# Windowed attention feeding a highway layer on one core: early v-buffer init, early sink rows, weights behind blocks 4 and 5, x of 15 blocks transposed by TensorE

## The chip, the core and the metric

The kernel runs on one core of a Trainium2 chip. Its time is the device time of one execution, in microseconds (us); a kernel's figure is the median of its runs. A run counts as slow when it is more than 1.5% above the fastest run of the same kernel. The profile is one execution. Its span, from the first to the last instruction, was about 1.7 us shorter than the time of the same execution.

## The reference

```python
# q, k, v: [4 batches, 8 heads, 768 positions, 64], float32; n_sink = 4, window = 128
scores = (q @ k.T) / 8
keep   = (key position < 4) | (0 <= query position - key position < 128)
a      = softmax(where(keep, scores, -1e9))
x      = (a @ v), heads side by side          # [3072 tokens, 512]
H, T   = relu(x @ w_h), sigmoid(x @ w_t + b_t)
out    = T * H + (1 - T) * x                  # [3072, 512], float32
```

The kernel cuts the tokens into 24 blocks of 128, six to a batch. A block needs its own keys and values, those of the block before, and the four "sink" keys and values at the start of the batch. Blocks 0 and 1 of a batch have the sinks inside their window, so the separate sink product starts at the third block of each batch (blocks 2, 8, 14, 20).

## The kernel before

TensorE (PE), VectorE (DVE), ScalarE (ACT), GpSimd (POOL) and SyncE (SP) each run their own list of instructions in order. An instruction that must wait holds back everything behind it in its list; the timeline of the kernel before, below, shows a memset that waits 9.3 us and the work held behind it. PSUM is the memory into which TensorE's products go in this kernel; "the crossbar" stands for a transpose made by a DMA transfer (`dma_start_transpose`), which SyncE issues.

GpSimd issues the loads of q, k and v, which convert to 16 bits on the way, and it also does small pieces of work on the sinks:

```python
NV = AHEAD + 4                                   # AHEAD = 8
v_ring = [const.tile([P, VW], FP16, ...) for i in range(NV)]      # 12 v buffers

# VectorE, at the very start
for vt in v_ring[0:3]:
    init_v(vt)                                   # the column of twos and the padding

# GpSimd, at the start:  loads 0, 1, 2 among the masks, then
load_v(2)
load_sink_v(0)
load_qk(3); load_v(3)
nc.gpsimd.dma_start(out=wt_sb, ...)              # the two weights
nc.gpsimd.dma_start(out=wh_sb, ...)
load_qk(4); load_v(4)
```

The main loop is a software pipeline. In iteration i it works on several blocks:

```python
for i in range(-2, NB + LAG + 1):                # LAG = 4, NB = 24
    m, o = i - LAG, i - LAG - 1
    if i == -2:
        warm_up(8); more_constants(); late_constants()
        for vt in v_ring[3:NV]:
            init_v(vt)                           # VectorE
        sink_ones(); sink_v(0)                   # sink_v: GpSimd makes the sink values
    act_sink(i)                                  # ACT, third block of a batch on, every second i
    pe_S(i + 1, 0); act_S(i + 1, 0); pe_S(i + 1, 1)     # scores, exp
    dve_d(o); dve_mask(i, 1)
    pe_T(i + 2)                                  # PE transposes q and k
    dve_e(o)
    pe_A(i)                                      # attention product, sinks included
    act_T(i + 2)                                 # ACT copies the transposes out of PSUM
    act_S(i + 1, 1); dve_mask(i + 1, 0)
    dve_rec(i); dve_o(o)                         # one reciprocal a block
    dve_x(i); sp_X(i)                            # x, and its transpose by DMA (crossbar)
    pe_Mt(m); act_u(m); pe_Mh(m)                 # the two highway products
    pe_sink(i + 1)                               # sink scores, every second i
    for n in ...: load_qk(n); load_v(n)          # 5 to 8 at i = -2, then n = i + 10
    if on(i + 2) and (i + 2) % NSC == 0:
        pool_sink((i + 2) // NSC)                # GpSimd: sink keys
    if i % NSC == 3: load_sink_v(i // NSC + 1)
    if i > 0 and i % NSC == 0: sink_v(i // NSC)  # GpSimd: sink values
# (conditions shortened)
```

The transposes of q and k, the highway products and the sink scores share two PSUM buffers, in rotation (`m_ps`, two buffers).

The softmax here doesn't subtract the row's maximum and nothing guards it: scores larger than these inputs give would overflow.

## Time and profile before

| | before |
|---|---|
| median of runs | 148.12 us (147.62 to 149.33, four runs) |
| span of the profile | 144.5 us |
| PE / DVE / ACT / POOL busy | 76 / 67 / 60 / 52% |
| reciprocal of block 0, block 4, block 23 | 29.2, 47.1, 128.5 us |

The reciprocals are good milestones: there is one a block, right after the block's attention product. The profiled run was a quick one (146.2 us of device time); over all calls the kernel before ranged from 145.8 to 152.3 us.

The page of the kernel before gives, under "busy tenths in 40 slices", how busy each engine was in each fortieth of the span (3.6 us), and further down the chain of work that ended last, as shares of the span:

```profile
PE   6645000190799999989999994899999999979930
DVE  6220000464066789988888995499889989988990
POOL 6989980399999959876746479641030000000000
DMA v<-in_v_dram 21%; POOL qsd L83 8%; POOL ksd L84 7%; PE tps L313 7%; PE hps L326 6%; POOL v L91 6%; PE av L279 6%; PE sps L245 3%; DVE dd L332 3%; DVE ee L338 2%; DVE otok L344 2%; ACT e L253 2%; PE av L285 2%; POOL vs L129 2%; PE tps L311 2%
```

PE is idle for long stretches up to slice 10 (36 us) and almost full from slice 12 on (slice 25 holds the longer of two waits for sink values). The list of waits (engine and line, what ended the wait, us in total, number of waits, longest) names the holes:

```profile
DVE v L94 <- DMA v<-in_v_dram: 18.4, 2, 9.3
PE av L279 <- DVE e L264: 15.5, 2, 14.7
PE sk L223 <- POOL ks L214: 4.4, 1, 4.4
PE av L285 <- POOL vs L129: 3.3, 2, 2.6
```

The timeline of the same kernel (start, duration, engine, line, operation, and in brackets the idle time before it with what ended it) shows the order:

```profile
17.56 0.95 POOL L91 DMA_DIRECT2D v<-in_v_dram  x1
18.17 0.07 DVE L94 MEMSET v<- 128x8 f16 x1 [9.34 <-DMA v<-in_v_dram]
27.27 0.07 DVE L94 MEMSET v<- 128x8 f16 x1 [9.01 <-DMA v<-in_v_dram]
28.24 0.93 PE L279 MATMUL av<-v,e 128*128 128x112 f16 x8 [14.72 <-DVE e L264]
36.96 1.03 PE L223 MATMUL sk<-qk,ks 128*128 128x128 f16 x8 [4.36 <-POOL ks L214]
47.13 0.21 DVE L293 RECIPROCAL rec<-av 128x8 f32<-128x8 f32 x1
```

Loads 3 and 4 were written in the program before the init of the buffers they fill, so the memsets had to wait until the loads landed: twice 9 us. The masks stand behind the memsets in VectorE's list, and the attention product behind the masks.

### The profile page before, as it was taken

The numbers are of one execution on the slowest core, as the hardware profiler recorded it, in microseconds if no ns is written. First come the engines' busy times: TensorE is split into PE (matmuls) and PEld (weight loads), VectorE is DVE, ScalarE is ACT, GpSimd is POOL, SyncE is SP. The second block draws the span as 40 slices with busy tenths as digits, with TensorE's granted clock in tenths as the row PEclk, the third lists the DMA queues.
The fourth block names the chain that finished last, engine by engine and source line by source line (L and its number), as shares of the span: only waits on it lengthen the run. The fifth ranks groups of instructions, "written<-read, shape, count | busy, mean of one in ns | idle before, by whom it ended". The sixth has DMA issues, their size and how long they took to land.

```text
span 144.5 us, 3130 instructions
## 1 busy us (share of the span) xinstructions
PE 109.9 (76%) x1216; PEld 70.4 (49%) x1216; DVE 97.0 (67%) x213; ACT 86.9 (60%) x105; POOL 75.8 (52%) x99
## 2 busy tenths in 40 slices
PE   6645000190799999989999994899999999979930
PEld 2234000180688566656765663567666666644400
DVE  6220000464066789988888995499889989988990
ACT  3058300061499869887886989198869888812210
POOL 6989980399999959876746479641030000000000
PEclk9999999999999999999999999999999999999998
DMA  1999999999999999999999999999943422634331
GB/s 11 111 134 105 119 173 169 86 96 147 160 156 155 153 134 194 196 186 163 179 187 187 182 185 161 140 178 195 185 119 109 113 90 79 54 111 128 126 145 73
DMA packets 92784, 20.14 MB, mean 139 GB/s; under 512 B 88673, under 2 KB 89697, under 8 KB 92770
## 3 DMA queue, kind: packets, MB, share of 16 engines
q0 software_dynamic: 76256, 10.51, 116.2%
q1 hardware_dynamic: 16514, 9.44, 31.3%
q8 instruction: 9, 0.15, 0.5%
q14 instruction: 5, 0.04, 0.1%
HBM read 21.01 MB, written 6.29 MB: 189 GB/s over the span
## 4 chain that ended last, share of the span: by engine, by line
PE 29%; POOL 25%; DMA 21%; issue 9%; DVE 8%; ACT 4%; POOLq 0%; DVEq 0%
DMA v<-in_v_dram 21%; POOL qsd L83 8%; POOL ksd L84 7%; PE tps L313 7%; PE hps L326 6%; POOL v L91 6%; PE av L279 6%; PE sps L245 3%; DVE dd L332 3%; DVE ee L338 2%; DVE otok L344 2%; ACT e L253 2%; PE av L285 2%; POOL vs L129 2%; PE tps L311 2%
## 5 line engine op out<-in xcount | busy, mean ns | idle before, releaser
L253 ACT ACTIVATE e<-sps,ebias 128x1024 f16<-128x1024 f32 (+1 forms) x48 | 49.8, 1042 | 19.8 <-PE sps L245 19.6
L279 PE MATMUL av<-v,e 128*128 128x112 f16 x352 | 25.4, 221 | 15.5 <-DVE e L264 15.5
L264 DVE TENSOR_TENSOR e<-e,mask 128x1024 f16<-128x1024 f16 (+1 forms) x48 | 31.1, 650 | 7.5 <-ACT e L253 7.1
L279 PEld LDWEIGHTS <-e 128*128 128x128 f16 x352 | 21.3, 102 | 21.0 <-DVE e L264 16.6
L205 ACT COPY qk<-tp 128x1024 f16<-128x1024 f16 x24 | 24.1, 1003 | 7.0 <-PE tp L200 7.0
L91 POOL DMA_DIRECT2D v<-in_v_dram x24 | 21.8, 910 | 10.2 <-DVE v L94 6.4
L84 POOL DMA_DIRECT2D ksd<-in_k_dram x24 | 21.7, 902 | 6.8 <-PE tps L313 3.4
L83 POOL DMA_DIRECT2D qsd<-in_q_dram x24 | 22.2, 925 | 4.9 <-DMA ksd<-in_k_dram 1.4
L326 PE MATMUL hps<-wh_sb,xT 128*128 128x512 f16 x96 | 24.6, 379 | 0.0
L313 PE MATMUL tps<-wt_sb,xT 128*128 128x512 f16 x96 | 24.6, 379 | 0.0
L319 ACT ACTIVATE u<-tps 128x512 f16<-128x512 f32 x24 | 14.4, 599 | 14.6 <-PE tps L313 14.6
L332 DVE SCALAR_TENSOR_TENSOR dd<-hps,xh 128x512 f16<-128x512 f32 x24 | 16.6, 690 | 7.4 <-PE hps L326 7.0
L245 PE MATMUL sps<-qk 64*128 64x128 f16 x352 | 16.0, 231 | 2.7 <-ACT qk L205 2.2
L338 DVE SCALAR_TENSOR_TENSOR ee<-u,dd 128x512 f16<-128x512 f16 x24 | 16.5, 686 | 0.5
L298 DVE TENSOR_TENSOR xh<-av,rec 128x512 f16<-128x512 f32 x24 | 16.4, 685 | 0.2
L245 PEld LDWEIGHTS <-qk 64*128 64x128 f16 x352 | 11.2, 100 | 9.9 <-issue 7.8
L344 DVE SCALAR_TENSOR_TENSOR otok<-xh,ee 128x512 f32<-128x512 f16 x24 | 15.6, 652 | 0.2
L326 PEld LDWEIGHTS <-xT 128*128 128x128 f16 x96 | 9.4, 98 | 11.8 <-issue 0.8
L313 PEld LDWEIGHTS <-xT 128*128 128x128 f16 x96 | 9.4, 98 | 9.2
L94 DVE MEMSET v<- 128x8 f16 x12 | 0.7, 65 | 18.4 <-DMA v<-in_v_dram 18.4
L285 PE MATMUL av<-vs,es 128*128 128x260 f16 x32 | 9.0, 281 | 3.3 <-POOL vs L129 3.3
L200 PE MATMUL tp<-ident,ksd 128*128 128x128 f16 x96 | 10.5, 238 | 1.1 <-DMA ksd<-in_k_dram 1.1
(45 smaller groups left out, 81.4 us busy)
## 6 DMA issues: line engine op xcount, KB each, us to landing
out_dram<-otok SPq DMA_DIRECT2D x24, 256.0 KB, 3.8
qsd<-in_q_dram POOLq DMA_DIRECT2D x24, 128.0 KB, 8.5
ksd<-in_k_dram POOLq DMA_DIRECT2D x24, 128.0 KB, 8.4
v<-in_v_dram POOLq DMA_DIRECT2D x24, 128.0 KB, 8.8
wt_sb<-in_moe_w_t_dram POOLq DMA_DIRECT2D x1, 512.0 KB, 7.6
wh_sb<-in_moe_w_h_dram POOLq DMA_DIRECT2D x1, 512.0 KB, 9.4
xT<-xh SPq DMA_TRANSPOSE x24, 7.0
vd<-in_v_dram POOLq DMA_DIRECT2D x4, 4.0 KB, 8.8
```

Of the source, the lines that this page charges most:

```text
L83: nc.gpsimd.dma_start(out=qsd, in_=q[b, :, rows, :].transpose([1, 0, 2]))
L84: nc.gpsimd.dma_start(out=ksd, in_=k[b, :, rows, :].transpose([1, 0, 2]))
L91: nc.gpsimd.dma_start(out=vt[:, :, 0:D], in_=v[b, :, rows, :].transpose([1, 0, 2]))
L205: nc.scalar.copy(out=qk, in_=tp_of.pop(n))
L245: nc.tensor.matmul(sps[:, hh, o:o + P], lhsT=kk[rows, hp, :], rhs=qT[rows, hp, :], start=True, stop=True)
L253: nc.scalar.activation(out=e.rearrange("p a b c d -> p a (b c d)"), in_=sps[:, :, 0:2 * np_ * P], func=AF.Exp, bias=ebias, scale=SCALE)
L264: nc.vector.tensor_tensor(out=ev, in0=ev, in1=m.unsqueeze(1).to_broadcast([P, 4, np_ * P]), op=ALU.mult)
L279: nc.tensor.matmul(av[:, g, 2 * hl + hh, 0:_AVN], lhsT=e[:, hh, hl, pc, :], rhs=vt[:, 65 * h:65 * h + _AVN], start=first, stop=False, skip ...
L313: nc.tensor.matmul(tps, lhsT=xT[:, kc, :], rhs=wt_sb[:, kc, :], start=False, stop=(kc == NOC - 1))
L326: nc.tensor.matmul(hps, lhsT=xT[:, kc, :], rhs=wh_sb[:, kc, :], start=(kc == 0), stop=(kc == NOC - 1))
L332: nc.vector.scalar_tensor_tensor(out=dd, in0=h_of.pop(n), scalar=0.0, in1=xh_of[n], op0=ALU.max, op1=ALU.subtract)
L338: nc.vector.scalar_tensor_tensor(out=ee, in0=u_of.pop(n), scalar=1.0, in1=dd_of.pop(n), op0=ALU.add, op1=ALU.mult)
```

## The change

Its intent is to free the start: initialise all v buffers before any load, fill the first sink rows before load 3, put the weights behind the loads of blocks 4 and 5, and keep the crossbar transposes of x away from the loads, by letting TensorE transpose x for as long as loads are running.

```diff
-        for vt in v_ring[0:3]:
+        for vt in v_ring:
             init_v(vt)
 ...
         load_sink_v(0)
-        load_qk(3)
-        load_v(3)
-        nc.gpsimd.dma_start(out=wt_sb, ...)
-        nc.gpsimd.dma_start(out=wh_sb, ...)
-        load_qk(4)
-        load_v(4)
 ...
+    def pe_X(n):
+        xtp = m_ps.tile([P, NOC, P], FP16, tag="m", name="xtp")
+        for j in range(NOC):
+            nc.tensor.transpose(xtp[:, j, :], xh_of[n][:, j * P:(j + 1) * P], ident)
+    def act_X(n):
+        nc.scalar.copy(out=xT, in_=xtp_of.pop(n))
+    def by_dma(n):
+        return n >= 15
 ...
-                for vt in v_ring[3:NV]:
-                    init_v(vt)
                 sink_ones()
-                sink_v(0)
 ...
             if on(i + 2):
                 pe_T(i + 2)
+            if on(i - 1) and not by_dma(i - 1):
+                pe_X(i - 1)
 ...
                 act_T(i + 2)
+            if on(i - 1) and not by_dma(i - 1):
+                act_X(i - 1)
 ...
                 dve_x(i)
-                sp_X(i)
+                if by_dma(i):
+                    sp_X(i)
 ...
+            if on(i + 2) and (i + 2) % NSC == 0:
+                pool_sink((i + 2) // NSC)
+                sink_v((i + 2) // NSC)
+            for n in (range(3, AHEAD + 1) if i == -2 else [i + 2 + AHEAD]):
                 ... load_qk(n), load_v(n) ...
+                if n == WAT:        # WAT = 4
+                    nc.gpsimd.dma_start(out=wt_sb, ...)
+                if n == WAT + 1:
+                    nc.gpsimd.dma_start(out=wh_sb, ...)
-            (pool_sink behind the loads; sink_v at i % NSC == 0)
-            if i >= 0 and i % NSC == 3 and b < B:
+            if i >= 0 and i % NSC == 1 and b < B:
                 load_sink_v(b)
```

More of the change, by code (lines that the diff above doesn't have):

```diff
@@ L60 @@
     LAG = 4
+    WAT = 4
     const = ctx.enter_context(tc.tile_pool(name="const", bufs=1))
@@ L155 @@
         load_sink_v(0)
-        load_qk(3)
-        load_v(3)
-        nc.gpsimd.dma_start(out=wt_sb, in_=moe_w_t.rearrange("(kc p) of -> p kc of", p=P))
-        nc.gpsimd.dma_start(out=wh_sb, in_=moe_w_h.rearrange("(kc p) of -> p kc of", p=P))
-        load_qk(4)
-        load_v(4)
     nc.sync.dma_start(out=bt32, in_=moe_b_t.unsqueeze(0))
@@ L191 @@
     qkT, tp_of, s_of, e_of, av_of, rec_of = {}, {}, {}, {}, {}, {}
+    xtp_of = {}
     xh_of, xT_of, t_of, u_of, h_of, dd_of, ee_of, sk_of = {}, {}, {}, {}, {}, {}, {}, {}
@@ L306, in sp_X @@
         xT_of[n] = xT
+    def pe_X(n):
+        xh = xh_of[n]
+        xtp = m_ps.tile([P, NOC, P], FP16, tag="m", name="xtp")
+        for j in range(NOC):
+            nc.tensor.transpose(xtp[:, j, :], xh[:, j * P:(j + 1) * P], ident)
+        xtp_of[n] = xtp
+    def act_X(n):
+        xT = x_pool.tile([P, NOC, P], FP16, tag="xT", name="xT")
+        nc.scalar.copy(out=xT, in_=xtp_of.pop(n))
+        xT_of[n] = xT
     def pe_Mt(n):
@@ L395 @@
                 pe_sink(i + 1)
-            first, last = (5, AHEAD) if i == -2 else (i + 2 + AHEAD, i + 2 + AHEAD)
-            for n in range(first, last + 1):
+            if on(i + 2) and (i + 2) % NSC == 0:
+                pool_sink((i + 2) // NSC)
+                sink_v((i + 2) // NSC)
+            for n in (range(3, AHEAD + 1) if i == -2 else [i + 2 + AHEAD]):
                 if n < NB:
@@ L400 @@
                     load_v(n)
-            if on(i + 2) and (i + 2) % NSC == 0:
-                pool_sink((i + 2) // NSC)
+                if n == WAT:
+                    nc.gpsimd.dma_start(out=wt_sb, in_=moe_w_t.rearrange("(kc p) of -> p kc of", p=P))
+                if n == WAT + 1:
+                    nc.gpsimd.dma_start(out=wh_sb, in_=moe_w_h.rearrange("(kc p) of -> p kc of", p=P))
             b = i // NSC + 1
-            if i >= 0 and i % NSC == 3 and b < B:
+            if i >= 0 and i % NSC == 1 and b < B:
                 load_sink_v(b)
-            if i >= 0 and i % NSC == 0 and i > 0 and i // NSC < B:
-                sink_v(i // NSC)
 _INS = ['q', 'k', 'v', 'n_sink', 'window', 'moe_w_h', 'moe_w_t', 'moe_b_t']
```

## The prediction

> **What bounds the kernel now.** The page gives a span of 144.5 us, in two regimes.
>
> *Start, to about 47 us: waits.* The timeline shows DVE idle from 8.8 to 18.2 and from 18.3 to 27.3 us: it initialises v buffers 3 and 4 only after their loads have landed (wait list: 18.4 us in 2 waits), and block 4's v load stands behind both weight loads (9.6 us to landing). No mask, so no attention product: PE idles 14.7 us. Then PE waits 4.4 us for the sink keys (GpSimd copies them at 36.4 us, behind the loads). The reciprocal of block 4 starts at 47.1 us.
>
> *From there: PE.* Reciprocals follow 3.75 to 4.35 us apart with PE busy throughout, the same with loads in flight (blocks 9-13) and without (20-22): DMA does not bound this stage. Exceptions: blocks 8 and 14 wait 0.8 and 2.6 us for sink values from GpSimd. After the last reciprocal (128.5 us) comes a DVE tail of 16 us.
>
> **Removed.** The 18.4 us DVE wait; the 4.4 us sink-key wait; the 0.8 and 2.6 us sink-value waits (values now made four blocks ahead); 15 of 24 crossbar transposes (off the path).
>
> **Added.** On PE four 128x128 transposes a block: the chain of waits shows 0.22 us for four that follow others. On ACT a 128x512 copy: half of the 1.0 us of the 128x1024 one, estimated 0.5 us; ACT then carries about 4.1 of a 4.6 us block. Both share two PSUM buffers with four other uses. Estimate: 0.3 us a block for the PE-bound iterations 5 to 15: +3.3 us. The Trainium skill ("TensorE: Matmul & The Clock Gate", Part 4) says that PE transposes end in PSUM and need a copy; the trace agrees.
>
> **Moved, and why the start is not worth 18 us.** GpSimd now fills sink values before load 3. It must wait for that small load (3.1 us to landing) and work 1.1 us, so load 3 is issued near 16 instead of 11.7 us. Estimated from 0.87 us per load and 6.4 us for both weights, k of blocks 3, 4, 5, 6 lands near 20.5, 23, 29, 34 us. Before, k 6 landed at 34.8: loading is not earlier, but blocks 0 to 3 are computed meanwhile. The load stream is the new limit of the start. Reciprocal 4 follows k 6, near 36.5 us: 47.1 - 36.5 = 10.6 us gained, less about 1 us because PE, idling on loads, still runs slow (four transposes take 0.61 us before 41 us, 0.40 after). The same page, Part 1, names about 3.4 us of sustained work before full rate; here it came about 5 us after PE resumed at 37.0.
>
> **Sum.** 10.6 - 1 - 3.3 + 3.4 = 9.7 us of the span; the tail is unchanged. 148.5 - 9.7, given rounding: **138.5 us**, 8 in 10 within **134.5 to 142.0**. Faster by over 2%: 0.96; within 2%: 0.03; slower: 0.01.
>
> **Right if the profile shows:** no DVE wait on v loads; first reciprocal near 13 us; GpSimd idle 2-3 us on the small sink load near 12 us; PE waiting for k 3 to 6 until about 34 us; reciprocal 4 at 35 to 38 us; blocks 5 to 14 at 4.3 to 4.7 us; no PE wait for sink values; the tail near 16 us.
>
> **Wrong if:** ACT sets the pace (blocks near 5 us: 142 or more); the weight loads push k 6 beyond 36 us; or loads land sooner without crossbar transposes among them (134 or less).

## The result

The changed kernel took 139.32 us (median of 139.12 to 139.38, four runs), against 148.12 us before. The ratio, here and below the mean time of a kernel's fast runs over that of the other's fast runs of the same rounds, so not quite the ratio of the quoted medians, is 0.939 (95% interval 0.933 to 0.945).

The same strips and the chain by line, from the page of the changed kernel (a slice is now 3.4 us):

```profile
span 137.6 us, 3217 instructions
PE   6657519829899799999997999999999999799910
POOL 6994799955969979999999991005000000000000
PE hps L334 11%; PE tps L321 11%; ACT e L249 9%; ACT qk L201 7%; DMA ksd<-in_k_dram 7%; PE av L275 5%; POOL qsd L84 5%; PE sps L241 4%; PE tps L319 4%; POOL ksd L85 4%; POOL v L92 4%; DVE dd L340 3%; DVE ee L346 3%; DVE otok L352 3%; PE sk L219 2%
```

The waits for v loads are gone, and two new names stand in the chain: the loads of k, and ACT. The list of waits of the changed kernel has, in place of the four lines above:

```profile
PE tp L194 <- DMA qsd<-in_q_dram: 4.0, 2, 2.6
PE tp L196 <- DMA ksd<-in_k_dram: 3.1, 5, 1.1
POOL vs L130 <- DMA vd<-in_v_dram: 2.7, 1, 2.7
PE tps L319 <- ACT qk L201: 2.1, 4, 0.7
```

Its timeline in the start:

```profile
11.24 0.58 POOL L127 DMA_DIRECT2D vd<-in_v_dram  x1
14.38 0.21 DVE L289 RECIPROCAL rec<-av 128x8 f32<-128x8 f32 x1 [0.84 <-PE av L275]
14.49 1.03 POOL L130 TENSOR_TENSOR vs<-vd,bm 32x512 f16<-32x512 f16 x1 [2.66 <-DMA vd<-in_v_dram]
15.48 0.95 POOL L84 DMA_DIRECT2D qsd<-in_q_dram  x1
35.82 0.40 PE L196 MATMUL tp<-ident,ksd 128*128 128x128 f16 x4 [0.43 <-DMA ksd<-in_k_dram]
37.50 0.21 DVE L289 RECIPROCAL rec<-av 128x8 f32<-128x8 f32 x1 [0.89 <-PE av L281]
```

Block 0 is done at 14.4 us instead of 29.2. GpSimd waits 2.66 us for the small sink load and then works on it, so load 3 goes out at 15.48 us; TensorE then follows the loads, and k of block 6 lands at 35.8 us.

Where the time went, read off the reciprocals:

| us | before | after |
|---|---|---|
| reciprocal of block 4 | 47.13 | 37.50 |
| from there to block 15, per block | 4.43 (4.13 without the two sink-value waits, 0.8 and 2.6 us) | 4.59 |
| block 15 to 23, per block | 4.07 | 4.13 |
| after the last reciprocal | 16.05 | 16.6 |

The start gave 9.6 us. The middle took 1.7 us back although its two waits (3.4 us) were gone. So the profiles differ by 6.9 us; the medians differ by 8.8 us because the profile of before was one of its quick runs.

The slower pace has this shape in the chain of the changed kernel (start, duration, what), here for one block of the middle:

```profile
48.09 0.35 PE sps L241 x8
48.47 1.11 ACT e L249
49.58 0.91 ACT qk L201
50.53 0.38 PE tps L319
50.91 0.86 PE tps L321 x4
51.77 0.86 PE hps L334 x4
```

Scores, exp, the copy of the q/k transposes, the highway products, and then the next scores (in every second block the sink scores come first): a ring of 4.5 us through both engines. In the kernel before, the chain from 64 to 73 us names PE alone.

### The profile page after: what moved, and what is told of

Same layout as the page of the kernel before. It is cut to its first block, busy times and chain, and to the rows that moved or that the text cites. A ratio compares the mean times of both kernels' runs of the same rounds, so it can differ in the third digit from the quotient of the medians.

```text
span 137.6 us, 3217 instructions
## 1 busy us (share of the span) xinstructions
PE 115.0 (84%) x1276; PEld 74.4 (54%) x1276; DVE 97.2 (71%) x213; ACT 94.1 (68%) x120; POOL 74.6 (54%) x99
## 4 chain that ended last, share of the span: by engine, by line
PE 43%; ACT 17%; POOL 15%; DMA 10%; DVE 8%; issue 3%; POOLq 0%; DVEq 0%
PE hps L334 11%; PE tps L321 11%; ACT e L249 9%; ACT qk L201 7%; DMA ksd<-in_k_dram 7%; PE av L275 5%; POOL qsd L84 5%; PE sps L241 4%; PE tps L319 4%; POOL ksd L85 4%; POOL v L92 4%; DVE dd L340 3%; DVE ee L346 3%; DVE otok L352 3%; PE sk L219 2%
## 5 line engine op out<-in xcount | busy, mean ns | idle before, releaser
L340 DVE SCALAR_TENSOR_TENSOR dd<-hps,xh 128x512 f16<-128x512 f32 x24 | 16.6, 690 | 12.6 <-PE hps L334 12.5
L334 PE MATMUL hps<-wh_sb,xT 128*128 128x512 f16 x96 | 24.6, 379 | 0.0
L321 PE MATMUL tps<-wt_sb,xT 128*128 128x512 f16 x96 | 24.6, 379 | 0.0
L275 PEld LDWEIGHTS <-e 128*128 128x128 f16 x352 | 21.9, 103 | 2.0 <-DVE e L260 1.2
L327 ACT ACTIVATE u<-tps 128x512 f16<-128x512 f32 x24 | 14.5, 602 | 10.6 <-PE tps L321 10.6
L241 PEld LDWEIGHTS <-qk 64*128 64x128 f16 x352 | 11.2, 99 | 11.5 <-issue 9.4
L294 DVE TENSOR_TENSOR xh<-av,rec 128x512 f16<-128x512 f32 x24 | 16.4, 684 | 0.2
L352 DVE SCALAR_TENSOR_TENSOR otok<-xh,ee 128x512 f32<-128x512 f16 x24 | 15.6, 651 | 0.2
L194 PE MATMUL tp<-ident,qsd 128*128 128x128 f16 x96 | 10.4, 236 | 4.2 <-DMA qsd<-in_q_dram 4.0
L289 DVE RECIPROCAL rec<-av 128x8 f32<-128x8 f32 x24 | 4.9, 204 | 12.1 <-PE av L275 6.7
```

Source lines behind the costliest of these rows:

```text
L241: nc.tensor.matmul(sps[:, hh, o:o + P], lhsT=kk[rows, hp, :], rhs=qT[rows, hp, :], start=True, stop=True)
L275: nc.tensor.matmul(av[:, g, 2 * hl + hh, 0:_AVN], lhsT=e[:, hh, hl, pc, :], rhs=vt[:, 65 * h:65 * h + _AVN], start=first, stop=False, skip ...
L321: nc.tensor.matmul(tps, lhsT=xT[:, kc, :], rhs=wt_sb[:, kc, :], start=False, stop=(kc == NOC - 1))
L334: nc.tensor.matmul(hps, lhsT=xT[:, kc, :], rhs=wh_sb[:, kc, :], start=(kc == 0), stop=(kc == NOC - 1))
L340: nc.vector.scalar_tensor_tensor(out=dd, in0=h_of.pop(n), scalar=0.0, in1=xh_of[n], op0=ALU.max, op1=ALU.subtract)
```

## The experiments

Each kernel was correct. "Reciprocal 4" is that of block 4 in the profile; the pace is the mean of blocks 5 to 15. Medians and ranges take all runs, the ratios fast runs alone. The changed kernel ran in the first call only, so every comparison with it below is between calls and chips; the fast runs of the kernel before averaged 148.3 us in its call and 146.6 to 147.2 us in the others. "Slow" is a matter of time alone here: the granted TensorE clock does not sort the runs (the kernel before took 145.8 us at 0.87 and 149.2 us at 0.985).

| kernel | median us (range) | ratio to before, 95% | reciprocal 4 | pace 5 to 15 |
|---|---|---|---|---|
| the changed kernel | 139.3 (139.1–139.4) | 0.939 (0.933–0.945) | 37.5 | 4.59 |
| init_only | 146.8 (145.0–149.0) | 0.997 (0.987–1.008) | 47.1, slow run | 4.67, slow run |
| init_late | 140.4 (138.8–140.9) | 0.954 (0.939–0.970) | 39.0, slow run | 4.60, slow run |
| weights_old | 142.2 (141.7–142.9) | 0.970 (0.958–0.982) | 41.0 | 4.60 |
| sink_late | 135.3 (134.5–136.1) | 0.924 (0.910–0.938) | 33.1 | 4.59 |
| x_all_crossbar | 143.3 (142.3–147.8) | 0.977 (0.968–0.985) | 39.0 | 4.95 |
| x_pe_first4 | 139.3 (136.9–140.1) | too few fast runs | 37.5, slow run | 4.70, slow run |
| x_all_pe | 142.8 (142.6–144.1) | 0.976 (0.968–0.984) | 37.2 | 4.59 |
| x_before_t | 137.9 (137.6–138.5) | 0.941 (0.936–0.947) | 37.4 | 4.52 |
| x_crossbar_sinkdve | 142.8 (141.0–143.7) | 0.966 (0.950–0.982) | 40.1, slow run | see below |
| crossbar_sinkdve2 | 137.4 (137.1–139.9) | 0.936 (0.923–0.949) | 40.4 | 4.23 |
| best_pe4 | 132.2 (129.0–134.3) | 0.881 (0.859–0.903) | 32.5, slow run | 4.39, slow run |
| best_mixed | 130.1 (129.1–130.9) | 0.885 (0.877–0.892) | 32.0 | 4.30 |

### 1. Who transposes x: x_all_crossbar, x_pe_first4, x_all_pe

One line is changed, to `n >= 0`, `n >= 4` and `n >= NB`:

```diff
     def by_dma(n):
-        return n >= 15
+        return n >= 0
```

> The changed kernel with every block transposed by the crossbar. Theory A (TensorE transposes are a cost: blocks 5 to 15 took 4.59 us each against 4.13 us without; the crossbar costs only where the load stream is the limit, up to block 6): k of block 6 lands 2 to 4 us later than 35.8, blocks 5 to 15 back at about 4.1 us, span about 135, time near 137 us, so a little faster than the changed kernel's 139.3. Rival B (the crossbar among the loads starves them all through, which is why the change took it away): slower than 139.3 us, blocks waiting for q and k loads after block 6.

> The changed kernel with TensorE transposes for blocks 0 to 3 alone, where TensorE waits for loads anyway. Theory A: k of block 6 still lands near 35.8 us, reciprocal 4 near 37.5, blocks 5 to 15 near 4.1 us: about 5 us less than the changed kernel, near 134.3 us. Rival B (crossbar starves the loads throughout): blocks after 5 wait for loads, time at or above 139 us.

> The changed kernel with all 24 blocks transposed by TensorE. Theory A: eight or nine more blocks at about 4.6 instead of 4.1 us: 3.5 to 4.5 us slower than the changed kernel, near 143 us. Rival B: no slower than 139.3 us, since fewer crossbar transfers.

x_all_pe did what theory A said: 142.8 us, and blocks 16 to 23 went from 4.13 to 4.55 us. So TensorE's transposes cost about 0.4 us in each block of the middle.

But x_all_crossbar, which has none of that cost, was 4 us slower than the changed kernel, where theory A expected 2 us faster. k of block 6 landed at 37.5 us, 1.7 us later, and from block 5 on its blocks ran at the old pace of 3.7 to 4.4 us, except block 12 (4.9 us) and block 8, which took 12.9 us. Rival B had the direction right, but not the mechanism: at block 8 TensorE was not waiting for q or k. The timeline of x_all_crossbar:

```profile
52.96 0.88 POOL L84 DMA_DIRECT2D qsd<-in_q_dram  x1
56.58 0.88 POOL L85 DMA_DIRECT2D ksd<-in_k_dram  x1 [2.74 <-DMA qsd<-in_q_dram]
58.31 0.46 POOL L210 COPY ks<-qk 64x16 f16<-64x16 f16 x2
58.83 1.03 PE L219 MATMUL sk<-qk,ks 128*128 128x128 f16 x8 [6.56 <-POOL ks L210]
```

TensorE waited 6.56 us for the copy of four sink keys, which took 0.46 us. (Block 8 grew by more than that, 8.6 us: between 57.5 and 63.3 us the granted clock was 0.5, and eight matmuls of the attention product took 0.95 us, not 0.56.) That copy stands in GpSimd's list behind load 13, and GpSimd was held within that load. In this trace GpSimd's loads take turns on eight completion semaphores, and nine of its ten waits for a DMA ended when the load eight earlier had landed. The chain of x_all_crossbar shows the one that held it:

```profile
44.83 10.90 DMA qsd<-in_q_dram
```

A q load took 10.9 us from issue to landing. With the crossbar among them the loads' median was 8.1 to 8.5 us, in the changed kernel 6.0 to 6.5. The Trainium skill ("DMA: Bandwidth & Descriptors", Issuing engines are not separate DMA queues) says that DMAs of all issuing engines run on the same 16 DMA engines and interleave; these figures agree. This suggested theory C: the crossbar hurts not by starving TensorE of data, but by delaying GpSimd, whose list holds the sink copies.

x_pe_first4 had the same kind of hole at block 14 (9.7 us instead of 4.3). Three of its four runs are slow, so its median decides nothing; its best, 136.9 us, is below the changed kernel's.

### 2. The parts of the change alone: init_only, init_late, weights_old

init_only is the kernel before with the first hunk of the diff and its counterpart (all twelve buffers initialised ahead):

> The kernel before with all v buffers initialised ahead and nothing else changed. Theory A (the vector engine's wait for loads was the plug; what is left is the sink keys behind the loads, and the sink value waits): no wait for v loads, TensorE waits for the sink keys until about 31 us, reciprocal 4 near 41 us instead of 47, blocks 5 to 15 at 4.1 us with the waits of 0.8 and 2.6 us still there; about 6 us under the kernel before, near 142 us. Rival (the load order is what matters, the init alone only moves the wait to the next load): within 2% of the kernel before.

It gained nothing: ratio 0.997. The profile (a slow run, 3% above the best) has no wait for v loads, but one of 17.5 us of TensorE for the sink keys, and reciprocal 4 at 47.05 us against 47.13 before. Its list of waits:

```profile
PE sk L223 <- POOL ks L214: 17.5, 1, 17.5
```

I had estimated that the sink copy would come at 31 us; it came at 36, where it had been before. The rival named the result ("only moves the wait"), though the next wait was the copy of the sink keys, which stands behind the loads of blocks 5 to 8. The change also moves that copy ahead of these loads; no run makes that move alone, so how much of the gain of the start it brings is not shown.

init_late is the changed kernel with the init back at its old place:

```diff
-        for vt in v_ring:
+        for vt in v_ring[0:3]:
             init_v(vt)
 ...
                 late_constants()
+                for vt in v_ring[3:NV]:
+                    init_v(vt)
                 sink_ones()
```

> The changed kernel with the init of v buffers 3 to 11 put back to its old place on the vector engine (after the late constants). Loads 3 and up are now written after it in the program, so no init can wait for a load. Theory: the early init is redundant once the loads have moved; time as the changed kernel, 139.3 us within 1%, no wait of the vector engine for v loads. Rival (the early place itself matters): first mask later by more than 1 us and time up by over 1%.

Its 140.4 us is within 1% of the changed kernel's 139.3, the list of waits names no wait of VectorE for v loads, the first reciprocal came at 14.5 us (14.4) and the pace was 4.60 us. Within this precision the early init, after which the change is named, does nothing once the loads stand behind it in the program. The profiled run was 1.5 us later at block 4, and its trace says why: k of block 6 landed at 35.9 us, as in the changed kernel, but from 35.8 to 39.0 us the granted clock was 0.50 (in the changed kernel 1.00 from 35 to 40 us), and eight matmuls of block 4's attention product took 0.95 us, not 0.56. The edit has no part in that.

weights_old puts both weights back behind load 3 (`if n == WAT - 1` for both):

> The changed kernel with both weight loads back behind load 3, where the kernel before had them. Theory (the same loads stand before k of block 6 either way): k 4 and k 5 about 6 and 3 us later, k 6 within 0.7 us of 35.8, reciprocal 4 within 1.5 us of 37.5, time within 1% of the changed kernel's 139.3. Rival (the place of the weights matters): over 2 us slower.

The theory fell: it was 2.8 us slower than the changed kernel. k of block 6 landed at 36.95 us, 1.2 us later, yet reciprocal 4 came 3.5 us later. Its timeline:

```profile
31.09 0.61 PE L194 MATMUL tp<-ident,qsd 128*128 128x128 f16 x4 [6.50 <-DMA qsd<-in_q_dram]
34.74 0.21 DVE L289 RECIPROCAL rec<-av 128x8 f32<-128x8 f32 x1 [8.48 <-PE av L281]
37.38 0.21 DVE L289 RECIPROCAL rec<-av 128x8 f32<-128x8 f32 x1 [0.47 <-PE av L281]
40.99 0.21 DVE L289 RECIPROCAL rec<-av 128x8 f32<-128x8 f32 x1 [0.24 <-PE av L281]
```

TensorE stood 6.5 us for q of block 4. From then on the loads came faster than blocks could be computed: k of blocks 4, 5 and 6 landed at 31.9, 34.4 and 36.95 us, while blocks 3 and 4 took 2.6 and 3.6 us, and block 6's transposes had to wait for their turn until 39.1 us. So it is not enough that the last load comes in time: the work must be spread between the loads, and that is what the weights behind blocks 4 and 5 do.

### 3. The small load in front of the large ones: sink_late

GpSimd's first `sink_v(0)` goes from before load 3 to after load 4:

```diff
                 pool_sink((i + 2) // NSC)
-                sink_v((i + 2) // NSC)
+                if i > -2:
+                    sink_v((i + 2) // NSC)
 ...
+                if i == -2 and n == 4:
+                    sink_v(0)
```

> The changed kernel with GpSimd's filling of the first sink values moved from before load 3 to after load 4, so that it need not wait for the small load. Theory D (the load stream limits the start): the 2.7 us wait of GpSimd goes, k of block 6 lands about 2.7 us earlier (near 33), reciprocal 4 near 35, the rest alike: about 2.5 us faster than the changed kernel, near 136.8. Rival (the backlog of the two weight loads sets when k 6 lands, not the issue of load 3): k 6 near 35.8 as before, time unchanged.

```profile
12.01 0.58 POOL L127 DMA_DIRECT2D vd<-in_v_dram  x1
12.58 0.92 POOL L85 DMA_DIRECT2D ksd<-in_k_dram  x1
16.98 1.23 POOL L130 TENSOR_TENSOR vs<-vd,bm 32x512 f16<-32x512 f16 x1
33.06 0.21 DVE L289 RECIPROCAL rec<-av 128x8 f32<-128x8 f32 x1 [1.71 <-PE av L281]
```

In this timeline of sink_late GpSimd has no wait left. k of block 6 landed at 31.3 instead of 35.8 us, reciprocal 4 came 4.4 us earlier at 33.1, and the median is 4.0 us below the changed kernel's: theory D holds, and the gain is larger than expected (the intervals of the two ratios just overlap, but the pace is the same 4.59 us, so the profiles place the whole gain in the start). I had counted GpSimd's 2.7 us of waiting alone. In the changed kernel, 4.6 us pass between the landing of the sink rows (14.3) and that of the next load (18.9); here 0.8 us (15.6 to 16.4). q of load 3 went out at 10.0 us instead of 15.5.

### 4. The pace with TensorE's transposes: x_before_t

```diff
-            if on(i + 2):
-                pe_T(i + 2)
             if on(i - 1) and not by_dma(i - 1):
                 pe_X(i - 1)
+            if on(i + 2):
+                pe_T(i + 2)
             # and the copies act_X, act_T likewise
```

> The changed kernel with TensorE's transposes of x put before those of q and k, and their copies likewise. Theory E (the extra 0.46 us per block is the rotation of two PSUM buffers: the t product takes the buffer of the q/k transposes and waits for their 0.9 us copy by ACT; with the order turned it waits for the shorter x copy): blocks 5 to 15 at about 4.35 instead of 4.59 us, the 0.3 us TensorE waits ahead of the t product gone, about 2.5 us faster than the changed kernel. Rival (ACT's or TensorE's work itself sets the pace): no change within 0.7 us.

Block by block (place in the batch: 0 to 5; reciprocal to reciprocal; blocks 12 to 15 and 10 to 11):

| us | 0 | 1 | 2 | 3 | 4 | 5 |
|---|---|---|---|---|---|---|
| before (blocks 16–17 and 18–21 where no wait disturbs) | 4.01 | 3.73 | 4.27 | 4.35 | 4.27 | 4.09 |
| changed kernel | 4.09 | 4.81 | 4.97 | 4.61 | 4.97 | 4.38 |
| x_before_t | 4.15 | 4.32 | 4.98 | 4.35 | 4.98 | 4.35 |

Theory E explains places 1 and 3, where the turned order saves 0.5 and 0.3 us; in place 3 the transposes then cost nothing. In places 2 and 4 nothing changed, so there the rival holds: the chain of x_before_t runs there from exp (1.11 us) through the copies of x (0.48) and q/k (0.92), the second exp (1.01) and tanh (0.50), all on ACT, to the sink scores:

```profile
57.90 1.11 ACT e L249
59.01 0.48 ACT xT L313
59.49 0.92 ACT qk L201
60.41 1.01 ACT e L249
61.42 0.50 ACT u L327
```

Block 8, not in the table, took 5.42 us, 0.44 more than in the changed kernel: TensorE waited 0.74 us there for the sink keys from GpSimd. Without it the saving is about 0.12 us a block instead of 0.07. The times of x_before_t overall, 137.9 us, are 2.5 us below init_late, but part of that is init_late's later start; the pace alone gives 11 x 0.07 = 0.7 us, which is the rival's limit. Theory E is a part of the cause, not the whole.

### 5. Is it GpSimd's list: x_crossbar_sinkdve and crossbar_sinkdve2

The crossbar does all transposes, and the sink copies of batches 1 to 3 move to VectorE. The small sink loads of these batches go out once, behind load 8.

```diff
-    def pool_sink(b):            # and sink_v(b)
+    def pool_sink(b, eng):       # and sink_v(b, eng): nc.gpsimd for batch 0, nc.vector after
-            nc.gpsimd.tensor_copy(out=dst[...], in_=kT[...])
+            eng.tensor_copy(out=dst[...], in_=kT[...])
 ...
     def by_dma(n):
-        return n >= 15
+        return n >= 0
```

> All blocks transposed by the crossbar, as in x_all_crossbar, but the sink keys and values of batches 1 to 3 are copied by the vector engine, and their rows loaded once near the start, so GpSimd's order no longer holds them. Theory C (crossbar transfers cost time because they lengthen each load's way to landing, GpSimd falls behind in its own order, and the sink copies come late; q, k, v themselves arrive in time): the 8.6 us extra at block 8 goes, blocks 5 to 23 at 3.7 to 4.4 us each, span near 133.5, time near 135.3. Rival B (TensorE lacks q and k themselves): a stall of similar length stays, near 143 us.

The hole at block 8 was gone (4.27 us), but block 5 took 9.6 us: I had made a new hole of the same kind. VectorE, in its own order, now waited for the small load:

```profile
46.50 0.68 DVE L130 TENSOR_TENSOR vs<-vd,bm 32x512 f16<-32x512 f16 x1 [5.25 <-DMA vd<-in_v_dram]
48.44 0.93 PE L275 MATMUL av<-v,e 128*128 128x112 f16 x8 [5.08 <-DVE e L260]
```

crossbar_sinkdve2 makes the sink values three blocks later, when the rows are there:

```diff
-                sink_v((i + 2) // NSC, eng)
+            if on(i) and i % NSC == 1 and i > NSC:
+                sink_v(i // NSC, nc.vector)
```

> x_crossbar_sinkdve mended: there the vector engine, in order, waited 5.3 us in block 4 for the small sink load that I had put behind load 8. Now it makes the sink values of batches 1 to 3 three blocks later, and their keys as before. All else as in x_all_crossbar. Theory C (crossbar transfers hurt only through GpSimd's late sink copies): no extra at block 8, blocks 5 to 23 at 4.1 to 4.2 us on average, reciprocal 4 near 39 to 40 us, span near 133.5, time near 135.5, so faster than the changed kernel without its TensorE transposes. Rival B (matmuls lack q, k, v): an extra of 5 us or more somewhere in blocks 5 to 14, near 141 us or more.

The median fell from x_all_crossbar's 143.3 to 137.4 us, with no TensorE transposes at all; that is 1.9 us below the changed kernel, though the ratios (0.936 and 0.939) do not separate the two. Block 8 took 4.28 us; blocks 5 to 23 averaged (119.57 - 40.35) / 19 = 4.17 us. So theory C holds for the large hole. Rival B is not quite empty: TensorE waited for k loads 6.7 us in all, in six waits, the longest 3.2 us in the start, and block 14 took 5.5 us. The sink loads moved together with the copies, so the two are not told apart.

### 6. Putting it together: best_pe4 and best_mixed

best_pe4 lets TensorE transpose x of blocks 0 to 3 alone, and gives all sink copies to VectorE (the sink rows of batches 1 to 3 are again loaded once, behind load 8):

```diff
-                pool_sink((i + 2) // NSC)
-                sink_v((i + 2) // NSC)
+                pool_sink((i + 2) // NSC, nc.vector)
+            if on(i) and i % NSC == 1:
+                sink_v(i // NSC, nc.vector)
 ...
-        return n >= 15
+        return n >= 4
```

> A version meant to beat both: TensorE transposes x of blocks 0 to 3 alone (there it waits for loads anyway), crossbar for the rest; all sink keys and values by the vector engine, so GpSimd issues loads alone after the prologue. If theories A, C and D hold: k of block 6 near 30.5 us, reciprocal 4 near 32.5, blocks 5 to 23 at 4.15 us on average, tail 16.3: span near 127.5, time near 129.5. If crossbar transfers starve the matmuls after all: an extra of several us in blocks 5 to 14, 134 or more.

Two of six runs hit the expected time (129.0 and 129.4 us); the others lay between 131.3 and 134.3. The profile, from one of the slower runs, shows TensorE waiting for keys:

```profile
73.39 0.40 PE L196 MATMUL tp<-ident,ksd 128*128 128x128 f16 x4 [0.84 <-DMA ksd<-in_k_dram]
79.31 0.40 PE L196 MATMUL tp<-ident,ksd 128*128 128x128 f16 x4 [1.68 <-DMA ksd<-in_k_dram]
```

With the early holes gone, TensorE takes a block every 4.1 to 4.2 us, and the loads among crossbar transfers come no faster: in this profile k of blocks 8 to 20 landed 4.54 us apart on average (3.71 us in best_mixed). best_mixed takes five more blocks from the crossbar, chosen at places where TensorE's transposes cost least (table above), and puts x before q and k:

```diff
-        return n >= 4
+        return n >= 4 and n not in (5, 8, 10, 11, 14)
```

> best_pe4 with TensorE transposing x of blocks 5, 8, 10, 11 and 14 too, and x put before q and k as in x_before_t. In best_pe4 TensorE waited 0.8 and 1.7 us for k of blocks 16 and 17, and four of six runs were 2 us or more above the best. Theory F (with the crossbar in every block the load stream keeps up only just, about 4.2 us for a block's three loads, and loses its lead by block 16): five fewer crossbar transfers keep the lead; no wait for k over 1 us after block 7, median near 129.3 us with a spread under 2.5 us, at a price of about 0.7 us in TensorE and ACT. Rival (those waits are one profile's noise): median and spread as best_pe4, 132 us and 5 us.

The median is 130.1 us and all six runs lie within 1.8 us; after block 7 the timeline has no wait for q or k. That is what theory F said of the waits and the spread, but two things were changed at once, and of best_pe4's four slow runs only one was profiled, so the cause of its spread is likely, not shown. By fast runs alone the two kernels are level (0.881 and 0.885), and the best run (129.1 us) is no faster than best_pe4's best. Its page:

```profile
span 127.9 us, 3185 instructions
PE   6646788398999999999999999999999999799920
```

best_mixed beats the kernel before by 11.5% and the changed kernel by about 9 us.

## Why the prediction was right or wrong

The predicted 138.5 us missed the measured 139.3 by less than 1%, and it was well inside the range. Not all of the reasons were right.

- **Right in sum: the start.** Predicted gain of the start 9.6 us (10.6 less 1); measured 47.13 - 37.50 = 9.63 us. First reciprocal 14.4 us (13 predicted), GpSimd's wait 2.66 us (2 to 3), k of block 6 at 35.8 us (near 34), reciprocal 4 at 37.5 (35 to 38). But the hit to the tenth is luck, because two misses cancel: k of block 6 landed 1.8 us later than estimated, and reciprocal 4 followed it after 1.7 us instead of 2.5 plus the 1 us taken off for a slow TensorE. It was not slow there: the granted clock was 0.51 from 31.0 to 34.4 us, but 1.00 when k of block 6 landed, and four transposes took 0.40 us at 35.8 us. (In the kernel before, matmuls ran at their quick rate again from 41.2 us, 4.2 us after TensorE resumed at 36.96.) sink_late shows that putting the sink rows in front of load 3 cost 4 us.
- **Incomplete: "the load stream is the new limit of the start".** weights_old shows that when k 6 lands does not decide alone; how the computing is spread between the loads counts too.
- **Not taken apart: the 18.4 us wait of VectorE.** The prediction names it first among what is removed. Removing it alone gives nothing (init_only), and with the loads moved the early init is not needed (init_late).
- **Mis-sized: 0.3 us a block for TensorE's transposes, 3.3 us in all.** Measured 0.46 us (4.59 against 4.13), 5.1 us over 11 blocks. The terms themselves were good: the ACT copy took 0.59 us (estimated 0.5). What I did not work out is the turn of the two PSUM buffers: with one more user, the highway product waits for the q/k copy, and a ring through PE and ACT sets the pace. x_before_t removes this in two of six places; in two more ACT's own list binds. So the rotation is a part of the 0.46 us, and ACT's added copy another; the runs do not give the shares.
- **Wrong: "15 of 24 crossbar transposes (off the path)".** This is the step that failed: the prediction gave their removal no worth. In the changed kernel, putting them back costs 4 us net, although it saves the 0.46 us a block (x_all_crossbar): GpSimd falls behind, and the sink copies with it. The prediction credited 3.4 us to sink copies made earlier in the program; at block 8 of x_all_crossbar, without TensorE's transposes, the early place did not help, and TensorE waited 6.56 us. Why the kernel before, with the same crossbar transfers, lost only 0.8 us at block 8 and 2.6 at block 14 was not tested.
- **Why the time still fitted.** By profiles the gain was 6.9 us, not 9.7: the middle lost 2.3 us more than predicted and the tail 0.6. Taken from the span of the profile, the prediction would have been 134.8 us, and the span was 137.6. The medians differ by 8.8 us because the timed runs of the kernel before were on the whole slower than its profiled run. So a part of the agreement is luck: I took a sum of one profile for a difference of medians.

What stays open is why the kernel before and the all-crossbar versions vary by 2.7 to 6.0 us within a call (the kernel before by 1.7 in the first), while the changed kernel varied by 0.3 in its one call. The kernels with few crossbar transfers among the loads vary less (x_all_pe 1.5, sink_late 1.7, best_mixed 1.8 us), but no run takes that apart, and the granted clock varied too, without sorting the runs.

## What to carry to other kernels

When an engine both issues loads and does small work, its list ties the work to the landing of loads issued long before; here a 0.5 us copy held TensorE for 6.6 us, and the cure was to move the copy to an engine that does not issue loads, placed so that its inputs had long landed. Removing the largest wait in a profile may only uncover the next one at the same time, so ask what stands behind it. And before adding a user to a PSUM rotation, write down whose copy out of PSUM each product will wait for: the added transposes, 0.22 us in the chain, do not account for the 0.46 us that a block grew.

## What the Trainium skill lacked or had wrong

- "DMA: Bandwidth & Descriptors", Rules for kernel authors, says that a transpose next to ordinary DMAs needs nothing. That held for correctness in all runs. No page gives its price to the loads: 8.1 to 8.5 us to landing with 24 crossbar transposes, 6.0 to 6.5 us with 9, at the end, in otherwise the same kernel.
- The same page, Anatomy of one DMA, fits about 2.0 us plus the bytes over 436 GB/s for a DMA issued by GpSimd. The 4 KB sink load took 3.1 us, and the first 128 KB loads, with little else in flight, 3.6 to 4.1 us, counted from the start of GpSimd's issuing instruction (itself 0.6 to 1.1 us). These loads convert from 32 to 16 bits, and the page has no figure for that.
- "TensorE: Matmul & The Clock Gate", Part 4, gives about 275 ns for a 128x128 transpose in a kernel and says that the full clock does not engage for it. Here the median was 219 ns, four in a row took 0.40 us where the trace grants the full clock (at 24.6 us in the changed kernel) and 0.61 us where it grants half of it (init_late, 35.8 to 39.0 us), and added only 0.22 us to the chain. It names a VectorE copy as the follow-up; here ACT made it, in 0.59 us.
- No page gives a figure for what an added user of a PSUM rotation does to the pace. Here the x transposes, 0.22 us in the chain, made a block 0.46 us longer; turning the order of two users took 0.07 us of that away, and the rest is not divided between the rotation and ACT's list.
